# Gathers of tokens in pairs half a step apart, and one at a time for the first expert, in a fused attention and mixture-of-experts kernel

## The chip, the cores and the metric

The kernel runs on one core of one Trainium2 chip. The metric is the device time of one execution in microseconds (us), the median of three runs. A profile of one more execution gives the rows that are shown here. Engines are named as the profile names them: PE is TensorE (matmuls; PEld its weight loads), DVE is VectorE, ACT is ScalarE, POOL is GpSimd, SP is SyncE, which issues most plain DMAs.

## The reference

A banded attention (8 batches, 8 heads, 576 positions, 64 values a head; half of the heads look at 32 neighbours, half at every fourth of 128) gives 4608 tokens of 512 values. A gate picks two of eight experts for each token, and each expert is two matrix products with a ReLU between them.

```python
x = attn_out.transpose(0, 2, 1, 3).reshape(4608, 512)
noisy_logits = x @ w_gate + np.log1p(np.exp(x @ w_noise)) * noise
top2 = np.argpartition(-noisy_logits, 2, axis=1)[:, :2]
...
for e in range(8):
    for k in range(2):
        mask = top2[:, k] == e
        h = np.maximum(x[mask] @ w1[e], 0.0)       # w1[e]: 512 x 1024
        out[mask] += top2_w[mask, k, None] * (h @ w2[e])   # w2[e]: 1024 x 512
```

## The kernel before

**Stages.** The first 176 us are the attention, in half-steps ("slots"); the change leaves them alone. The attention's output `x` goes to a scratch tensor `xs` in HBM. Then come the eight experts. The first takes its tokens while the gate of the last quarter is still being worked out; the other seven are taken in the order of their load.

**One expert.** Its tokens are cut into tiles of 128, nine or ten of them, and these into three blocks of three or four tiles. For a block, `up` makes eight products (one for each 128 of the 1024 hidden values) of 12 matmuls each; ACT writes the ReLU of a product from PSUM to `hh`, DVE the remainder to `hl` (fp32 is split into two parts to be multiplied). Three PSUM buffers, named `up`, hold products that ACT and DVE have not read yet. Then `down` makes, for each tile, 24 matmuls into `dn` (two buffers), DVE scales the result to `y` (three buffers), and POOL adds `y` to the output in HBM by an indirect DMA (`scatter`). Blocks of one expert are interleaved with those of the one before.

**Tokens.** A tile's tokens are fetched by POOL with indirect DMAs (`gather`), into one of four buffers `g`. For the first expert a tile is two DMAs of 128 x 256 values; for the others four DMAs of 128 x 128, each for 32 tokens. `xsplit` turns a fetched tile round (on DVE for the seven, on PE for the first expert), ACT casts it to `x`, and DVE writes the remainder. Which tokens belong to an expert is worked out on DVE and PE by products with 0/1 matrices (`zero_one` writes `lo` and `hi`, `add_up` multiplies them into `plc`), six of them for each expert, and POOL writes the index lists `ixi`.

**Order.** The order is written out by the program. `plan(t, f)` puts a step into a heap under a due time; `tick(cols)` moves a clock by the matmul columns just issued and calls what is due, so a step lands on its engine's queue between two matmuls of the program. Every queue is in order. A position in the queue is no time yet: POOL runs ahead as far as its waits allow.

**Pacing.** `pace` puts a tiny instruction into POOL's queue: a 1x1 copy from the latest `hh` (`late["x"]`), so that POOL waits until ACT has written it, or a memset where no wait is asked for. The name of its target is `spacer`. In the kernel before, one such copy stands ahead of the four gathers of a tile, a memset ahead of every scatter, and `gpsimd.nop()` ahead of the first expert's gathers once the experts have begun. The first expert's gathers are taken by `first_blocks`, a generator that `some` advances: `new_slot(2)` allows two gathers, and `some` is planned at 34 steps of one microsecond of the program's clock. `drain` ends what is left.

Of the kernel before, what the change touches and what calls it, by code (L numbers as in the profile page):

```python
# [9 lines left out]
F32 = mybir.dt.float32  # L10
# [30 lines left out]
US_W2 = 3.0, 3.5  # L41
US_W2S = 0.5, 2.4, 8.6, 10.6
LAG = 15
US_X = (17, 46)
WIN = (0.5, 19, 23, 27, 31, 35), (0.5, 6.3, 12.1, 17.9, 23.7, 29.5)
LAGS = (6, 3.9, 3.9, 3.9, 3.9, 3.9), (5.7,) * 6

# [2 lines left out]
def attention_moe_kernel(ctx, tc, qt, kp, kd, vpl, vdl, wgn, noise, w1, w2, out, CAPS=(1184, 1216, 1216, 1184, 1184, 1152, 1152, 1152), SPLITS=(0, 384, 768)):  # L50
    nc = tc.nc
    tensor, vector, scalar, gpsimd, sync = nc.tensor, nc.vector, nc.scalar, nc.gpsimd, nc.sync
# [3 lines left out]
    TLS = [[(128 * i, min(128, cap - 128 * i)) for i in range((cap + 127) // 128)] for cap in CAPS]  # L56
# [16 lines left out]
    gp_ = ctx.enter_context(tc.tile_pool(name="gp", bufs=4))  # L73
# [239 lines left out]
    gens, early, behind = [], [True], [True]  # L313
    room, held, rate = [0], set(), [1]

    fresh, backlog, mark = [True], [], [None]

    def new_slot(scatters, speed=1):
        if scatters:
            room[0], fresh[0], mark[0] = scatters, True, late["x"]  # L320
        rate[0] = speed
        held.clear()

    def pace(yes=True, at=None):

        at = late["x"] if at is None else at
        if yes and at is not None:
            gpsimd.tensor_copy(spacer, at)  # L328
        else:
            gpsimd.memset(spacer, 0.0)  # L330

    def pool_turn():


        if experts[0]:
            gpsimd.nop()
        else:
            pace(fresh[0], mark[0])
        fresh[0] = False
        room[0] -= 1  # L340

# [5 lines left out]
    def micro(n=1):  # L347

        n = (1, n, 2 * n)[rate[0]]
        for g in list(gens):
            while n > 0 and g not in held:
                try:
                    r = next(g)
                except StopIteration:
                    gens.remove(g)
                    break
                n -= 1
                if r == 1:  # L360
                    held.add(g)
                if r == 3:
                    break
# [522 lines left out]
    GT, GOT = {}, {}  # L886

    def gather(e, t, c=None):
        r0, rn = TLS[e][t] if e != "o" else (0, 128)
        if e == 0:  # L890

            GOT[t] = c == 1
            if c == 0:
                GT[e, t] = gp_.tile([128, 4, 128], F32, name="g")
            rows = 2304 * (next((i for i in range(U - 1) if r0 + rn <= SPLITS[i]), U - 1) + 1)
            gpsimd.indirect_dma_start(
                out=GT[e, t][0:rn, 2 * c:2 * c + 2].rearrange("p c d -> p (c d)"), out_offset=None, in_=xs[0:rows],
                in_offset=bass.IndirectOffsetOnAxis(ap=IX[0][0][0:rn, t, c:c + 1], axis=0))
            return
        g = gp_.tile([128, 4, 128], F32, name="g")  # L900
        if e != "o":
            pace()
        for j in range(rn // 32):
            gpsimd.indirect_dma_start(out=g[:, j], out_offset=None, in_=xq,  # L904
                                      in_offset=bass.IndirectOffsetOnAxis(
                                          ap=IX[e][1][:, r0 // 32 + j:r0 // 32 + j + 1], axis=0))
        GT[e, t] = g
# [22 lines left out]
    def new_x(e, bi):  # L930
        pool = late["xp0" if bi == 0 else "xp"]
        t = pool.tile([128, 2, 4, NBL[bi]], F32R, name="x", tag="raw" if bi == 0 else f"x{bi}")
        X[e, bi] = (t[:, 0], t[:, 1])

    def plan_x(e, bi, t, step, lag):
        plan(t, lambda: new_x(e, bi))
        for i, ti in enumerate(range(BLS[e][bi][0], BLS[e][bi][1])):
            plan(t + step * i, lambda ti=ti: gather(e, ti))
            plan(t + step * i + lag, lambda ti=ti: xsplit(e, bi, ti), 1.2)

    HT = {}
# [116 lines left out]
    def plan(t, f, lag=None):  # L1058

        if lag is not None:  # L1060
            plan(t, lambda: plan(now[0] + lag, f()))
        else:
            heappush(due, (t, next(turn), f))
# [27 lines left out]
    experts, done = [False], [0, 0, 0]  # L1091
# [18 lines left out]
    def split_first(bi, t):  # L1110
        if GOT.get(t) and (0, t) in GT:
            xsplit(0, bi, t)()
            done[bi] += 1

    def x_block(bi):
# [4 lines left out]
        for i, t in enumerate(range(BLS[0][bi][0], BLS[0][bi][1])):  # L1120
            plan(US_X[bi - 1] + 3.0 * i, lambda t=t: split_first(bi, t))

# [44 lines left out]
    for kc in range(4):  # L1167
        a, b, c = ((-3, 2.5, 3), (-2, 4.5, 5), (2, 7.5, 8), (2, 7.5, 8))[kc]
# [61 lines left out]
        gate_turn(*f, last=2)()  # L1230
    micro(14)

    def some():
        new_slot(2)
        micro(8)

    def drain():
        while gens:
            some()


    actx.close()
# [14 lines left out]
    def dur(e, bi, dn, a=0, b=9):  # L1257
        t0, t1, s0, n = BLS[e][bi]
        st = tail(e, bi)
        if (a, b) != (0, 9):  # L1260
            n, st = 128 * (min(b, t1 - t0) - a), 0
        return (96 * n if not dn else 24 * 4 * (n - st) + 8192 * (st > 0)) / 2400.0
# [6 lines left out]
    for e in range(E):  # L1269
        first, last = e == 0, e == E - 1  # L1270
        order = [(0, 0, e), (1, 2, e - 1), (0, 1, e), (1, 0, e), (0, 2, e), (1, 1, e)]
        if first:

            order = [(0, 0, 0), (1, 0, 0), (0, 1, 0), (1, 1, 0), (0, 2, 0), (1, 2, 0)]
        elif e == 1:
            order = [(0, 0, 1), (1, 0, 1), (0, 1, 1), (0, 2, 1), (1, 1, 1)]
        t, at_ = start, {}
        for dn, bi, x, *ab in order:
            at_[dn, bi] = t
            t += dur(x, bi, dn, *ab)  # L1280
        end = t
        t = start if e < 2 else at_[0, 1]
        if not first:
            plan(t - 6, lambda e=e: (stage_w2(EID[e], 0), stage_w2(EID[e], 1)))
        turns = [US_W2[0] + US_W2[1] * c for c in range(4)] if first else US_W2S
        for c in range(4):
            plan(t + turns[c], lambda c=c: split_w2(c), 1.2)
            if c < 2 and not first:
                plan(t + turns[c] + 0.1, lambda c=c, e=e: stage_w2(EID[e], c + 2))
        if first:  # L1290
            half = late["hp"].tile([128, 8, 512], F32, name="half", tag="hh")
            for c in range(2):
                stage_w2(0, c + 2, half[:, 2 * c:2 * c + 2])
            plan(0, lambda: new_x(0, 1))

            def last_gate(before):
                while any(g in gens for g in before):
                    yield 1
                yield from gate(NT - NG, NG)
                plan(now[0] + 4, lambda: new_x(0, 2))  # L1300
                list_block(2)
                yield 0
                yield from totals()

            gens.append(last_gate([g for g in gens if g.__name__ == "turn_by_turn"]))
            for i in range(34):
                plan(start + i, some)
            plan(start + 33.5, drain)
            plan(start + 35, numbers)
            experts[0] = True  # L1310
        else:
            plan_x(e, 2, start + 2, *((7.5, 17) if e == 1 else (9, LAG)))
        if not last:
            if first:
                t = plan_places(1, start + 34.5, [3.9 * b for b in range(6)], (3.85,) * 6)
            t = max(ready.pop(0), start + 29, at_[0, 1]) if ready else t
            if e + 2 < E:
                ready.append(plan_places(e + 2, at_[1, 2] + 6 if first else at_[1, 1] + 7.5, WIN[first], LAGS[first]))
            plan_x(e + 1, 0, t, *((6, 13) if first else (9, LAG)))
            plan_x(e + 1, 1, t + (18 if first else 27), *((6, 13) if first else (9, LAG)))  # L1320
            t = at_[0, 2] + dur(e, 2, False)
            plan(t - 8, lambda e=e: (stage_w1(EID[e + 1], 0), stage_w1(EID[e + 1], 1)))
            for c in range(4):
                plan(t + 0.5 + 3 * c, lambda c=c: split_w1(c), 1.2)
                if c < 2:
                    plan(t + 0.6 + 3 * c, lambda c=c, e=e: stage_w1(EID[e + 1], c + 2))
        for dn, bi, x, *ab in order:
            if dn:
                down(x, bi, *ab)
            else:  # L1330
                while e == 0 and done[bi] < BLS[0][bi][1] - BLS[0][bi][0]:
                    some()
                    for t in range(*BLS[0][bi][0:2]):
                        split_first(bi, t)
                up((e, bi), X.pop((e, bi)), BLS[e][bi][3], tail(e, bi))
        start = end
# [7 lines left out]
    with tc.If(big > 0):  # L1344
        with tc.For_i(0, E, 1) as r:
            e = nc.values_load(ci[0:1, bass.ds(r, 1)], min_val=0, max_val=E - 1)
# [92 lines left out]
```

## Time and profile before

| | us |
|---|---|
| median of 3 runs | 1041.82 |
| lowest and highest run | 1040.22, 1042.13 |
| the profiled execution, its own time | 1046.44 |
| its span, first to last instruction | 1044.6 |
| PE busy in the span | 1007.8 |
| DVE, POOL, ACT busy | 572.1, 482.3, 319.9 |

The profiled execution took 4.62 us more than the median run, and 1.84 us of its time lie outside its span. PE is busy for 96% of the span.

### The profile page before, as it was taken

Reading aid. Unit: us, or ns where it says so; the run is one execution under the profiler, and the core shown is the slowest. Engines: PE = TensorE matmul, PEld = TensorE weight load, DVE = VectorE, ACT = ScalarE, POOL = GpSimd, SP = SyncE. Lnnn points to the kernel's source line nnn. Section 1 sums busy time; section 2 is a strip of 40 time slices with the busy share of each in tenths; the row PEclk is TensorE's granted clock in tenths of the full one; section 3 lists DMA queues with packets and bytes.
Section 4 is the critical chain, followed back from the end, with each engine's and each line's share of the span. In section 5 each row is a group of like instructions: output and inputs, shape, how many; then the busy total and the mean of one; then the engine's idle time right before and its main releaser. Section 6 shows DMA issues by size and latency. Waiting matters only on the chain.

```text
span 1044.6 us, 20009 instructions
## 1 busy us (share of the span) xinstructions
PE 1007.8 (96%) x7773; PEld 889.0 (85%) x7776; DVE 572.1 (55%) x1445; ACT 319.9 (31%) x605; POOL 482.3 (46%) x665
## 2 busy tenths in 40 slices
PE   7999999989999999999999999999999999999996
PEld 4778877888988988988988997899799988999885
DVE  6766867846486364736463557345644574444211
ACT  6765767311231231313121312232222212322010
POOL 5000020341787676565546554764376437653113
PEclk9999999999999999999999999999999999999999
DMA  7998987741364162345234433443343425344213
GB/s 307 347 346 307 313 315 259 290 99 22 74 154 94 31 142 51 86 86 112 60 74 96 94 83 54 109 93 81 50 119 80 98 47 122 82 95 90 31 18 45
DMA packets 58643, 132.03 MB, mean 126 GB/s; under 512 B 11216, under 2 KB 20944, under 8 KB 57264
## 3 DMA queue, kind: packets, MB, share of 16 engines
q1 hardware_dynamic: 38544, 92.02, 26.4%
q0 software_dynamic: 20000, 38.69, 20.9%
q8 instruction: 62, 1.02, 0.4%
q14 instruction: 37, 0.30, 0.1%
HBM read 91.93 MB, written 38.73 MB: 125 GB/s over the span
## 4 chain that ended last, share of the span: by engine, by line
PE 70%; issue 8%; DVE 7%; DMA 6%; POOL 3%; ACT 2%; another core or an unknown queue 2%; SPq 0%; POOLq 0%; DVEq 0%; ACTq 0%
PE up L985 31%; PE dn L1027 28%; DMA qt<-in_qt 2%; PE o L444 2%; PE s L397 2%; POOL g L904 2%; POOL out_rows L1004 1%; DMA out_rows<-y,ixs 1%; PE pp L426 1%; DMA xs<-x 1%; PE plc L756 1%; PE xtp L479 1%; DVE lo L745 1%; PE pp L501 1%
## 5 line engine op out<-in xcount | busy, mean ns | idle before, releaser
L985 PE MATMUL up<-x,w1h 128*128 128x384 f32 (+2 forms) x1536 | 401.2, 342 | 3.8 <-DVE hl L991 3.0
L904 POOL DMA_INDIRECT g<-xs,ixi x258 | 266.4, 1033 | 80.3 <-issue 77.2
L985 PEld LDWEIGHTS up<-x,w1h 128*128 128x128 f32 x1536 | 280.6, 189 | 8.6 <-DVE hl L991 3.3
L985 PE MATMUL up<-x,w1l 128*128 128x384 f32 (+2 forms) x768 | 262.2, 341 | 0.0
L1027 PE MATMUL dn<-w2h,hh 128*128 128x512 f32 x568 | 224.7, 396 | 0.0
L991 DVE SCALAR_TENSOR_TENSOR hl<-up,hh 128x384 fp32r<-128x384 f32 x192 | 106.7, 556 | 212.9 <-ACT hh L989 156.5
L1027 PE MATMUL dn<-w2l,hh 128*128 128x512 f32 x568 | 221.9, 391 | 0.5 <-DVE w2l L872 0.5
L1027 PE MATMUL dn<-w2h,hl 128*128 128x512 f32 x568 | 222.1, 391 | 0.0
L989 ACT ACTIVATE hh<-up 128x384 fp32r<-128x384 f32 (+2 forms) x192 | 95.2, 499 | 322.8 <-PE up L985 237.8
L1004 POOL DMA_INDIRECT out_rows<-y,ixs x66 | 105.6, 1600 | 141.2 <-DVE y L1036 103.7
L985 PEld LDWEIGHTS up<-x,w1l 128*128 128x128 f32 x768 | 145.4, 189 | 1.0
L1027 PEld LDWEIGHTS dn<-w2h,hl 128*128 128x128 f32 x568 | 107.0, 188 | 23.0
L1027 PEld LDWEIGHTS dn<-w2l,hh 128*128 128x128 f32 x568 | 107.1, 188 | 21.8 <-DVE w2l L872 0.9
L1027 PEld LDWEIGHTS dn<-w2h,hh 128*128 128x128 f32 x568 | 107.1, 189 | 20.7
L1036 DVE TENSOR_SCALAR y<-dn,ixs 128x512 f32<-128x512 f32 x62 | 46.5, 749 | 134.5 <-PE dn L1027 97.2
L926 ACT CAST x<-xr 128x512 fp32r<-128x512 f32 x67 | 40.5, 604 | 204.2 <-DVE xr L924 174.6
L763 POOL TENSOR_SCALAR ixi<-ixs 32x10 int32<-32x10 int32 (+1 forms) x112 | 35.5, 317 | 53.5 <-DVE ixs L709 43.6
L328 POOL COPY spacer<-hh 1x1 f32<-1x1 f32 x67 | 24.9, 372 | 71.9 <-ACT hh L989 71.1
L745 DVE TENSOR_TENSOR lo<-il,spob 128x384 bf16<-128x384 bf16 x84 | 46.2, 550 | 15.1 <-PE plc L756 10.8
L681 POOL TENSOR_TENSOR hi<-dat,hot 128x540 bf16<-128x540 bf16 (+1 forms) x4 | 3.5, 873 | 108.9 <-DVE dat L669 94.7
L927 DVE TENSOR_TENSOR x<-xr,x 128x512 fp32r<-128x512 f32 x67 | 44.7, 667 | 7.7 <-ACT x L926 4.9
L924 DVE STREAM_TRANSPOSE xr<-g 128x512 f32<-128x512 f32 x67 | 45.7, 682 | 1.1 <-DMA g<-xs,ixi 1.1
(239 smaller groups left out, 1053.8 us busy)
## 6 DMA issues: line engine op xcount, KB each, us to landing
ws<-in_moe_w SPq DMA_DIRECT2D x34, 512.0 KB
ws<-in_moe_w SPq DMA_DIRECT2D x112, 128.0 KB
out_rows<-zero SPq DMA_DIRECT2D x38, 256.0 KB
vd<-in_vdl SPq DMA_DIRECT2D x24, 390.0 KB
vp<-in_vpl SPq DMA_DIRECT2D x16, 585.0 KB
qt<-in_qt SPq DMA_DIRECT2D x14, 576.0 KB
xs<-x SPq DMA_DIRECT2D x24, 256.0 KB
kt<-in_kd SPq DMA_DIRECT2D x16, 320.0 KB
```

Of the source, the lines that this page charges most:

```text
L745: vector.tensor_tensor(lo[:, a:a + 3], il.unsqueeze(1).to_broadcast([128, 3, 128]), spob[:, 0, t].unsqueeze(2).to_broadcast([128, 3, 128]) ...
L763: gpsimd.tensor_scalar(xi[32 * c:32 * c + 32].rearrange("p (t g) -> p g t", g=4)[:, g, 0:n], ti[32 * g:32 * g + 32, 0:n, c // 2], 2.0, flo ...
L904: gpsimd.indirect_dma_start(out=g[:, j], out_offset=None, in_=xq, in_offset=bass.IndirectOffsetOnAxis(ap=IX[e][1][:, r0 // 32 + j:r0 // 32 ...
L924: vector.transpose(xr[:, :, 0:rn].rearrange("p c (g t) -> p g c t", t=32), g[:, 0:n].rearrange("p g (c d) -> p g c d", d=32))
L926: scalar.copy(xh[:, :, o:o + rn], xr[:, :, 0:rn])
L927: return lambda: vector.tensor_tensor(xl[:, :, o:o + rn], xr[:, :, 0:rn], xh[:, :, o:o + rn].bitcast(F32), op=OP.subtract)
L985: tensor.matmul(p[:, 0:n], lhsT=a[:, 128 * f:128 * f + 128], rhs=b[:, kc, 0:n], start=(i == 0), stop=(i == 11))
L989: scalar.activation(hh[:, f, 0:n], p[:, 0:n], AF.Relu)
L991: vector.scalar_tensor_tensor(hl[:, f, 0:m], p[:, 0:m], 0.0, hh[:, f, 0:m].bitcast(F32), op0=OP.max, op1=OP.subtract)
L1004: ins = gpsimd.indirect_dma_start(out=out, out_offset=bass.IndirectOffsetOnAxis(ap=sc[0:rn, t, 1:2], axis=0), in_=y[0:rn], in_offset=None, ...
L1027: tensor.matmul(p[0:rn], lhsT=a[:, f, o:o + rn], rhs=b[:, f % 2], start=(i == 0), stop=(i == 23))
L1036: vector.tensor_scalar(y[0:rn], p[0:rn], wsc, None, op0=OP.mult)
```

## The change

Three things change. For experts two to eight the four gathers of a tile no longer stand together: `plan_x` plans two of them at the tile's time and two half a step later, and each pair has its own `pace`. For the first expert every single gather has a `pace` ahead of it also after the attention, so that it waits for a product's `hh`. And `some` allows one gather at every second call in place of two at every call, is planned 48 times in place of 34, and `drain` no longer waits for the gathers; the times at which the first expert's second and third block are turned round (`US_X`) move by 2 and 3 us.

```diff
-US_X = (17, 46)
+US_X = (19, 49)
...
     def pool_turn():
-        if experts[0]:
-            gpsimd.nop()
-        else:
-            pace(fresh[0], mark[0])
+        pace(fresh[0], mark[0])
         fresh[0] = False
         room[0] -= 1
...
-        g = gp_.tile([128, 4, 128], F32, name="g")
+        if c:
+            g = GT[e, t]
+        else:
+            g = gp_.tile([128, 4, 128], F32, name="g")
         if e != "o":
             pace()
-        for j in range(rn // 32):
+        for j in range(rn // 32) if c is None else range(2 * c, min(2 * c + 2, rn // 32)):
...
         for i, ti in enumerate(range(BLS[e][bi][0], BLS[e][bi][1])):
-            plan(t + step * i, lambda ti=ti: gather(e, ti))
+            for c in range(2 if TLS[e][ti][1] > 64 else 1):
+                plan(t + step * (i + c / 2), lambda ti=ti, c=c: gather(e, ti, c))
             plan(t + step * i + lag, lambda ti=ti: xsplit(e, bi, ti), 1.2)
...
+    calls = count()
     def some():
-        new_slot(2)
+        new_slot(1 - next(calls) % 2)
         micro(8)
     def drain():
-        while gens:
-            some()
+        while any(g.__name__ != "first_blocks" for g in gens):
+            new_slot(0)
+            micro(8)
...
-            for i in range(34):
+            for i in range(48):
                 plan(start + i, some)
```

The first place is POOL's queue where the first expert's third block is fetched, after the second scatter of that expert. `g` are the tiles, `hh_3394` the ReLU of its first block, `hh_3824` that of its second. Before:

```order
L1004 DMA out_rows<-y_3721,ixf_1984 4864x512
L896 DMA g_3794<-xs_57,ixf_1984 128x256 x2
L896 DMA g_3811<-xs_57,ixf_1984 128x256 x2
L896 DMA g_3823<-xs_57,ixf_1984 128x256 x2
L896 DMA g_3850<-xs_57,ixf_1984 32x256 x2
L1003 MEMSET spacer_184 1x1
L1004 DMA out_rows<-y_3768,ixf_1984 4864x512
```

And of the change, from the third of the eight gathers on:

```order
L328 COPY spacer_184<-hh_3394 1x1
L893 DMA g_3840<-xs_57,ixf_1984 128x256
L328 COPY spacer_184<-hh_3824 1x1
L893 DMA g_3840<-xs_57,ixf_1984 128x256
L328 COPY spacer_184<-hh_3824 1x1
L893 DMA g_3954<-xs_57,ixf_1984 128x256
L328 COPY spacer_184<-hh_3824 1x1
L893 DMA g_3954<-xs_57,ixf_1984 128x256
L328 COPY spacer_184<-hh_3824 1x1
L893 DMA g_4001<-xs_57,ixf_1984 32x256
L328 COPY spacer_184<-hh_3824 1x1
L893 DMA g_4001<-xs_57,ixf_1984 32x256
```

Eight gathers and a scatter with nothing between them but a memset have become eight gathers with a copy ahead of each, the last five of which read the second block's `hh`, which is being written product by product; the scatter of `y_3768` follows them.

The second place is POOL's queue about the last `up` and the first `down` of the third expert (the same piece comes again for the later ones). Before:

```order
L328 COPY spacer_184<-hh_6404 1x1
L904 DMA g_6512<-xs_57,ixi_5372 128x128 x4
L1003 MEMSET spacer_184 1x1
L1004 DMA out_rows<-y_6370,ixs_4481 4864x512
L328 COPY spacer_184<-hh_6404 1x1
L904 DMA g_6595<-xs_57,ixi_5372 128x128 x4
L1003 MEMSET spacer_184 1x1
L1004 DMA out_rows<-y_6558,ixs_4481 4864x512
```

And of the change:

```order
L328 COPY spacer_184<-hh_6428 1x1
L904 DMA g_6537<-xs_57,ixi_5383 128x128 x2
L328 COPY spacer_184<-hh_6428 1x1
L904 DMA g_6537<-xs_57,ixi_5383 128x128 x2
L1004 MEMSET spacer_184 1x1
L1005 DMA out_rows<-y_6394,ixs_4484 4864x512
L328 COPY spacer_184<-hh_6428 1x1
L904 DMA g_6621<-xs_57,ixi_5383 128x128 x2
L1004 MEMSET spacer_184 1x1
L1005 DMA out_rows<-y_6584,ixs_4484 4864x512
L328 COPY spacer_184<-hh_6428 1x1
L904 DMA g_6621<-xs_57,ixi_5383 128x128 x2
```

Each four have become two and two, the second pair of the first tile has moved behind the end of `up` (its copy reads the last product's `hh`), and the second pair of the second tile stands behind the scatter of `y_6584`, which waits for the first `down` of the block.

## Rows read from the trace of the kernel before

**Rows 1.** The page: the span, and the group of the gathers of experts two to eight

```profile
span 1044.6 us, 20009 instructions
L904 POOL DMA_INDIRECT g<-xs,ixi x258 | 266.4, 1033 | 80.3 <-issue 77.2
```

**Rows 2.** PE in order of time: start, us, tile, count, idle time before and its end

```profile
226.50 0.62 PE L985 MATMUL up<-x,w1h 128*128 128x384 f32 x2 [2.97 <-DVE hl L991]
320.01 0.28 PE L756 MATMUL plc<-hi,lo 128*128 128x90 bf16 x3 [0.76 <-DVE hi L749]
361.12 0.65 PE L985 MATMUL up<-x,w1h 128*128 128x448 f32 x2 [0.81 <-issue]
406.75 0.28 PE L756 MATMUL plc<-hi,lo 128*128 128x90 bf16 x3 [0.73 <-DVE hi L749]
408.39 0.28 PE L756 MATMUL plc<-hi,lo 128*128 128x90 bf16 x3 [1.35 <-DVE hi L749]
523.25 0.28 PE L756 MATMUL plc<-hi,lo 128*128 128x90 bf16 x3 [1.27 <-DVE hi L749]
```

**Rows 3.** Who waited for whom: us in total, times, longest

```profile
DVE y L1036 <- remote: 24.2, 7, 6.9
ACT hh L989 <- remote: 20.7, 5, 7.5
...
PE plc L756 <- DVE hi L749: 7.9, 7, 1.4
```

**Rows 4.** The chain that ended last: start, us, what

```profile
215.20 2.09 PE up L985 x12
217.86 7.48 another core or an unknown queue
226.50 8.08 PE up L985 x36
...
256.83 2.27 PE up L985 x12
...
408.67 5.80 PE dn L1027 x18
414.74 4.18 PE dn L1027 x18
```

**Rows 5.** ACT and DVE in order of time, where they ran late

```profile
225.36 1.25 ACT L989 ACTIVATE hh<-up 128x384 fp32r<-128x384 f32 x3 [7.50 <-remote]
...
359.71 0.54 ACT L989 ACTIVATE hh<-up 128x448 fp32r<-128x448 f32 x1 [5.92 <-remote]
...
519.91 0.56 DVE L745 TENSOR_TENSOR lo<-il,spob 128x384 bf16<-128x384 bf16 x1 [2.18 <-PE dn L1027]
```

**Rows 6.** POOL in order of time, first and last of two strings of transfers

```profile
212.46 1.02 POOL L896 DMA_INDIRECT g<-xs,ixf  x1 [0.30 <-issue]
...
222.46 1.63 POOL L1004 DMA_INDIRECT out_rows<-y,ixf  x1 [0.22 <-issue]
...
508.37 0.97 POOL L904 DMA_INDIRECT g<-xs,ixi  x1 [0.48 <-issue]
...
519.20 0.96 POOL L904 DMA_INDIRECT g<-xs,ixi  x1 [0.30 <-issue]
```

**Rows 7.** Busy time in two stretches: PE, PEld, DVE, ACT, POOL, granted clock, DMA

```profile
227.90:231.20 3.30, 3.30 (x12) 3.30 (x11) 3.25 (x14) 0.49 (x1) 0.00 (x0) 0.50 0.18 65
408.80:412.10 3.30, 3.30 (x9) 2.61 (x8) 2.03 (x6) 0.00 (x0) 2.38 (x3) 0.50 0.14 40
```

**Rows 8.** POOL and DVE: the one tile turned round as soon as it landed

```profile
347.99 0.94 POOL L904 DMA_INDIRECT g<-xs,ixi  x1 [0.30 <-issue]
...
350.54 0.71 DVE L924 STREAM_TRANSPOSE xr<-g 128x512 f32<-128x512 f32 x1 [1.12 <-DMA g<-xs,ixi]
```

**Rows 9.** POOL, a copy between gathers that waited for nothing

```profile
444.44 0.18 POOL L328 COPY spacer<-hh 1x1 f32<-1x1 f32 x1
444.78 0.97 POOL L904 DMA_INDIRECT g<-xs,ixi  x1 [0.16 <-issue]
```

## The prediction

> **What bounds the kernel now.** I read the page first: the span is 1044.6 us [rows 1], PE is busy for 1007.8 us of it by the table above, and the chain of work that ended last runs along PE's two product lines from 176 us on. What can be gained there is PE's idle time and the time in which its clock is low. So I went through PE in order of time from 165 us to the end and kept each idle piece over half a microsecond. There are ten; the first, 0.55 us ahead of a weight remainder, has nothing to do with the gathers, the nine others are these: 2.97 us at 226.5, 0.81 at 361.1, and seven waits of `plc` for DVE's `hi` [rows 2], which the view of waits sums up as 7.9 us [rows 3]. Six of these seven are seen to belong together: 0.73 and 1.35 at 406 to 408, and one near 523, 631, 739 and 845, of which the first (1.27) is shown [rows 2].
>
> Then I asked what was late. At 215.20 PE begins the first expert's second `up`, one product every 2.09 us [rows 4], so the second product is done at 215.20 + 2 x 2.09 = 219.4. ACT reads it at 225.36, together with the next two [rows 5]: 6 us late, though ACT stood idle (7.50 us). PE, with three PSUM buffers, stops at 223.5. The view of waits calls such an end "remote", a signal whose sender it cannot tell: five times for ACT (20.7 us), seven times for DVE's `y` (24.2 us) [rows 3]. The reader is to see what POOL does meanwhile: from 212.46 to the scatter at 222.46 it issues nine indirect transfers, one every 1.25 us, with no wait between them [rows 6], and the signal comes some microseconds after that string ends. At 359.71 ACT is late in the same way [rows 5]. At 519.91 DVE's `lo` starts late on a signal of PE [rows 5], in a string that began at 508.37 and whose last gather is at 519.20 [rows 6]; `hi` follows `lo`, and PE pays 1.27 us at 523.25 [rows 2]. So PE's signals arrive late inside long strings of POOL's transfers. That is a coincidence seen many times, not a mechanism that the trace shows.
>
> **The clock.** [...] The price is in the chain: 36 `up` matmuls take 8.08 us where 12 take 2.09, so 8.08 - 6.27 = 1.81 us; 18 `dn` matmuls take 5.80 where the same take 4.18, so 1.62 us [rows 4].
>
> **The change, part by part.**
>
> *First expert.* The string of eight gathers and a scatter goes. The first three copies read an `hh` that is long written and wait for nothing; the five others wait for a product each, and products are 2.09 us apart [rows 4], so one transfer leaves per product. The last gather is issued near 229 and must be turned round and split before the third block's `up` at 256.83 [rows 4]; a gather is seen to be read 2.55 us after its issue (347.99 to 350.54) [rows 8]. More than 20 us are left, so this delay costs nothing. The scatter behind it comes some 8 us later, and its `y` buffer is asked for only in the block after. Gain if the late signal goes: 2.97 + 1.81 = 4.78 us.
>
> *Pairs.* The same 258 gathers [rows 1] leave in strings of two, and in `up` each pair waits for its own product, so POOL gets a pause between pairs: two gathers take 2.5 us, half a step is 3 to 4.5 us by the numbers with which `plan_x` is called. In `down` the copies wait for nothing, since no new `hh` is written; there the scatters, which wait for `y`, break the string. By the second place of the change the string 508.37 to 519.20 becomes a pair, a pause until the last product's `hh`, then pair, scatter, pair, a scatter that waits. Gains if the signals come in time: 0.81 us at 361.1; 0.73 + 1.35 + 1.62 = 3.70 us at 406 to 412; and the four like 523, which are 7.9 - 0.76 - 0.73 - 1.35 = 5.06 us [rows 2, 3]. The 0.76 us at 320 lie in a stretch where DVE itself is full, and I leave them.
>
> *Price on POOL.* The built program has 77 more instructions on POOL, nearly all copies. A copy that waits for nothing puts 0.34 us between two gathers (444.44 to 444.78) [rows 9] where 0.30 stand without it [rows 6]; one that waited adds 0.18 + 0.48 = 0.66 [rows 6, 9]. That is 3 to 51 us on an engine that idles 1044.6 - 482.3 = 562 us, and it holds nobody up by itself. Zero is my value; the other end comes in by the next part.
>
> *Price of later data.* The second half of a tile is planned 3 to 4.5 us later, while the turning-round keeps its place: 13 to 17 us after the first half. Ten microseconds are left in which POOL has to get to the pair, issue it (2.5 us) and land it (2.55 us). So POOL may be 5 us behind before DVE stands. It has been 4 us behind once, where DVE stood 1.12 us [rows 8] and PE lost nothing. Value: zero; the other end is below.
>
> Sum: 4.78 + 0.81 + 3.70 + 5.06 = 14.35 us. Against the profiled execution that is 1046.44 - 14.35 = 1032.1. The median of the runs is 4.62 us lower, and profiling may be part of these very stalls: then 14.35 - 4.62 = 9.73 us are left in a run, 1041.82 - 9.73 = 1032.1; if none is, 1041.82 - 14.35 = 1027.5. I take the middle: **1030 us**, own range 1026 to 1035.
>
> [...]
>
> **The rivals.**
>
> *Only the first expert is cured.* In `down` a pair's copy waits for nothing; pair, scatter, pair there are still five transfers, and it is in `down` that `plc` waits. Then 2.97 + 1.81 + 0.81 = 5.59 us are won: 1041.82 - 5.59 = 1036.2 us. For it: the late signal at 519.91 lies in such a stretch. Against: the string there was nine transfers long and had begun in `up`. Chance 0.18.
>
> *The strings are not the cause, or only under the profiler.* Signals stay late, or were never late in a run: 1041.8 us. For it: no row shows how a transfer of POOL could hold a signal of PE. Against: ACT's late hits all lie inside or right behind such strings [rows 3, 5, 6]. Chance 0.12.
>
> *Slower: the second pairs come too late.* DVE's queue is in order; when `xr` waits for a pair, the `hl` behind it waits, and ACT and PE after three products. It decides once POOL is over 5 us behind at a pair, which it can be behind a scatter that waits for a `y` from a `down` of 5.5 us, or behind the index lists. The price is that of the lateness which DVE now has near 519.91: 2.18 us of idle DVE [rows 5] made 1.27 us of PE [rows 2]. If one tile of each of three blocks of seven experts were hit so, 21 x 1.27 = 26.7 us would be lost against the 14.35 won: 1041.82 + 12.3 = 1054 us; with one tile in an expert 7 x 1.27 = 8.9 us, against only the first expert's 4.78: 1046 us, which I take. Chance 0.12.
>
> [...]
>
> **How the numbers follow.** The forecast has 0.58, the rivals 0.18, 0.12 and 0.12. The median's three runs spread by 0.18%, so 0.2% (2.1 us) is about what a measurement here can tell from no change: faster means below 1039.7. Nearly all of the first two cases is faster: 0.57 + 0.17 + 0.01 = 0.75; the same 0.13, slower 0.12. The range goes from 1026, a little under the full sum with the 0.76 us at 320 added (1026.7), up to 1041, which leaves out the slower case and half of the third: under 0.2.
>
> **What would show it.** Right: PE has no idle piece near the end of the first expert's second `up`, the granted clock stays at 1.00 after it and near 408; the five "remote" waits of ACT and the seven of `y` go from tens of microseconds to a few; `plc`'s 7.9 us for `hi` shrink to about one; POOL's busy time grows by little and its strings have two or three transfers. Second rival's sign: `plc` still waits some 1.2 us an expert. Slower: DVE's `xr` waits for `g` many times, not once. The prediction is wrong if late signals are there beside short strings, or if they go and the runs stay at 1041.

## The result, and the profile after

The change takes 1032.05 us (median of 6 runs, 1028.30 to 1034.46); the kernel before took 1041.97 us in the runs beside it (6 runs, 1040.22 to 1047.35). The ratio is 0.9888, interval 0.9859 to 0.9917. But the gain depends on the chip: on another one the same two kernels stand at 0.9993 (0.9965 to 1.0021), and the kernel before takes 1030.05 us there.

First the chip of the first traces. The page of the change, its span, its engines and the group of the gathers:

```profile
span 1032.0 us, 20122 instructions
## 1 busy us (share of the span) xinstructions
PE 1002.2 (97%) x7773; PEld 884.3 (86%) x7776; DVE 573.4 (56%) x1445; ACT 319.7 (31%) x605; POOL 499.8 (48%) x742
...
L904 POOL DMA_INDIRECT g<-xs,ixi x258 | 266.2, 1032 | 81.8 <-issue 78.4
```

A gather takes 1032 ns, where [rows 1] have 1033; POOL is busy for 17.5 us more, and the span is 12.6 us shorter.

PE of the change in order of time. After the attention these are all its idle pieces over half a microsecond (start, us, tile, count, idle time before and its end):

```profile
202.88 0.50 PE L1028 MATMUL dn<-w2l,hh 128*128 128x512 f32 x1 [0.81 <-DVE w2l L869]
317.09 0.28 PE L753 MATMUL plc<-hi,lo 128*128 128x90 bf16 x3 [0.53 <-DVE hi L746]
318.13 0.28 PE L753 MATMUL plc<-hi,lo 128*128 128x90 bf16 x3 [0.76 <-DVE hot L744]
```

Of [rows 2] only the 0.76 us near 320 is left, which the prediction left out, with 0.53 us beside it. The view of waits of the change, against [rows 3]:

```profile
DVE y L1037 <- remote: 13.7, 2, 7.1
ACT hh L990 <- remote: 5.8, 2, 3.5
...
DVE xr L924 <- DMA g<-xs,ixi: 1.3, 2, 1.1
PE plc L753 <- DVE hi L746: 1.0, 2, 0.5
```

The "remote" ends fell from 20.7 and 24.2 us to 5.8 and 13.7, `plc`'s wait from 7.9 us to 1.0, and `xr` waits for its tokens hardly more than before (1.3 us; 1.12 in [rows 8]). The 13.7 us of `y` are not the "few" that the prediction named as a sign. The two stretches of [rows 7], in the windows that answer to them (PE, PEld, DVE, ACT, POOL, granted clock, DMA):

```profile
216.00:235.00 19.00, 18.57 (x115) 18.01 (x114) 11.70 (x35) 3.92 (x8) 9.06 (x16) 1.00 0.52 116
400.00:420.00 20.00, 20.00 (x107) 15.51 (x106) 15.08 (x38) 1.24 (x2) 15.65 (x19) 1.00 0.38 66
```

PE is busy for 18.57 of 19.00 us and for all of 20.00, and its clock is 1.00 in both. To see where the time came from, read the start of the same PE instruction in several traces. Times from the first expert's first `up`:

| PE begins | before | change | before on chip 10 |
|---|---|---|---|
| first `up` (its own time) | 0 (176.33) | 0 (178.69) | 0 (177.79) |
| first expert, second `up` | 38.71 | 37.85 | 37.14 |
| first expert, second `down` | 61.36 | 55.68 | 54.97 |
| second expert, second `down` | 192.08 | 186.78 | 184.26 |
| third expert, second `up` | 250.93 | 241.61 | 239.09 |
| fourth | 359.72 | 348.98 | 346.46 |
| fifth | 467.29 | 455.17 | 452.65 |
| sixth | 574.95 | 561.36 | 558.85 |
| seventh | 677.12 | 662.18 | 659.66 |
| last `down` | 826.44 | 811.50 | 808.98 |

The gain comes in steps at the places of [rows 2]: 4.82 us at the first expert, 4.02 before the third expert's second `up`, then 1.42, 1.38, 1.47 and 1.35, and none behind the seventh expert's second `up`. The last column is the kernel before, unchanged, on another chip: it is shorter still.

The strings themselves did not all become short. Count as one string the transfers of POOL with gaps under 0.7 us between them: the kernel before has 20 strings of seven or more, with 222 of its 356 transfers, and the change has 21, with 230. The first expert's string is gone. At the place of 523 there is still one, of ten transfers, since its scatters do not wait (PE's first `down` matmul, DVE's reading of that tile, then the first gather, the first scatter and the last gather of the string):

```profile
506.17 0.39 PE L1028 MATMUL dn<-w2h,hh 128*128 128x512 f32 x1
...
512.17 0.75 DVE L1037 TENSOR_SCALAR y<-dn,ixs 128x512 f32<-128x512 f32 x1 [0.32 <-PE dn L1028]
...
507.65 1.11 POOL L904 DMA_INDIRECT g<-xs,ixi  x1 [0.48 <-issue]
...
510.68 1.61 POOL L1005 DMA_INDIRECT out_rows<-y,ixs  x1 [0.22 <-issue]
...
521.99 1.01 POOL L904 DMA_INDIRECT g<-xs,ixi  x1 [0.26 <-issue]
```

And in the kernel before:

```profile
513.13 0.39 PE L1027 MATMUL dn<-w2h,hh 128*128 128x512 f32 x1
...
521.40 0.75 DVE L1036 TENSOR_SCALAR y<-dn,ixs 128x512 f32<-128x512 f32 x1 [0.35 <-remote]
```

What changed is when the string begins: 4.76 us ahead of `down` before (508.37 in [rows 6]), 1.48 us behind its start now, because its first pair waits for the last product's `hh`. The first tile is done 5.96 us into `down`. Eight transfers of the string had been issued by then before, three are now, and DVE reads the tile 0.04 us after its end where it took 2.3 us. At the three later places like it the counts are the same, eight and three.

A reader's lateness is the time from the end of what it reads, or from the end of the reader's own work before if that is later. Of 270 reads of a product or a `down` tile, 17 are late by over 0.3 us in the kernel before (31.36 us together, 6.00 at most) and 10 in the change (14.55 us, 2.71 at most), all ten behind seven or more transfers of a string. So the change made late signals fewer, and those that are left fall where PE does not stop for them; it did not end them.

### The profile page after: what moved, and what is told of

Same layout as the page of the kernel before. It is cut to its first block, busy times and chain, and to the rows that moved or that the text cites. A ratio compares the mean times of both kernels' runs of the same rounds, so it can differ in the third digit from the quotient of the medians.

```text
span 1032.0 us, 20122 instructions
## 1 busy us (share of the span) xinstructions
PE 1002.2 (97%) x7773; PEld 884.3 (86%) x7776; DVE 573.4 (56%) x1445; ACT 319.7 (31%) x605; POOL 499.8 (48%) x742
## 4 chain that ended last, share of the span: by engine, by line
PE 78%; issue 8%; DVE 6%; POOL 3%; DMA 3%; ACT 1%; another core or an unknown queue 0%; SPq 0%; POOLq 0%; DVEq 0%; ACTq 0%
PE up L986 33%; PE dn L1028 31%; PE o L441 4%; PE s L394 3%; PE pp L423 2%; POOL out_rows L1005 1%; PE xtp L476 1%; PE pp L498 1%; PE plc L753 1%; DMA out_rows<-y,ixs 1%; POOL g L904 1%; PE dn L1022 1%; PE dn L1024 1%; PE s L383 1%; PE pp L540 1%
## 5 line engine op out<-in xcount | busy, mean ns | idle before, releaser
L904 POOL DMA_INDIRECT g<-xs,ixi x258 | 266.2, 1032 | 81.8 <-issue 78.4
L1005 POOL DMA_INDIRECT out_rows<-y,ixs x66 | 110.8, 1679 | 100.5 <-DVE y L1037 76.8
L328 POOL COPY spacer<-hh 1x1 f32<-1x1 f32 x144 | 49.6, 345 | 131.1 <-ACT hh L990 129.1
L855 DVE TENSOR_TENSOR w1l<-ws,w1h 128x1024 fp32r<-128x1024 f32 x32 | 38.8, 1222 | 16.7 <-issue 11.8
```

The source lines that it names most:

```text
L1005: ins = gpsimd.indirect_dma_start(out=out, out_offset=bass.IndirectOffsetOnAxis(ap=sc[0:rn, t, 1:2], axis=0), in_=y[0:rn], in_offset=None, ...
```

## The experiments

Results name their chip by a number; each kernel is timed beside the kernel before on the same chip. The signs to look for are the time of the kernel before, the "remote" waits, and the semaphore records that a trace holds: counted over the whole trace, 9,320 in the first trace of before and 9,931 in that of the change.

**The parts, chip 5.** `e1_first_alone` is the kernel before with the lines of the diff on the first expert:

```diff
-        if experts[0]:
-            gpsimd.nop()
-        else:
-            pace(fresh[0], mark[0])
+        pace(fresh[0], mark[0])
...
-        new_slot(2)
+        new_slot(1 - next(calls) % 2)
```

> The kernel before with the part on the first expert alone: one gather at a time, each behind a copy; experts two to eight keep their four gathers together. Theory (long strings of POOL's transfers hold back PE's signals until the string ends): PE's idle 2.97 us and the half clock behind it go, nothing else; the trace of the whole change was 4.82 us shorter than that of before over that stretch, so 1041.97 - 4.8 = 1037.2 us, ratio 0.995 to 0.996, and plc still waits for hi near 523, 631, 739 and 845. Rival (only the first expert counts, the pairs bring nothing): the whole gain, ratio 0.989.

`e2_pairs_alone` is the kernel before with the other lines:

```diff
-            plan(t + step * i, lambda ti=ti: gather(e, ti))
+            for c in range(2 if TLS[e][ti][1] > 64 else 1):
+                plan(t + step * (i + c / 2), lambda ti=ti, c=c: gather(e, ti, c))
```

> The kernel before with the pairs alone: experts two to eight as in the change, the first expert's gathers still in strings. Theory: PE keeps the idle piece of about 3 us and the half clock near 226; the stops at 406 to 412 and the four later ones go, in the traces 3.98 + 5.62 us, and some 1 us before: ratio 0.990 to 0.992. Rival (only the first expert counts): ratio 0.998 to 1.000, and plc waits as before.

`e3_pairs_together`, from the change:

```diff
-                plan(t + step * (i + c / 2), lambda ti=ti, c=c: gather(e, ti, c))
+                plan(t + step * i, lambda ti=ti, c=c: gather(e, ti, c))
```

> The whole change, but both pairs of a tile are planned at the tile's own time, each with its copy. Both copies then read the same hh, so that the second waits for nothing and the string is four transfers long again, with a copy of 0.18 us in its middle. Theory (what counts is the pause between strings): as the first-expert part alone, ratio 0.995 to 0.996, late signals back at the later experts. Rival (any instruction with a semaphore between two transfers lets the signals through): ratio as of the whole change, 0.989.

`e4_pairs_untied`, from the change:

```diff
         if e != "o":
-            pace()
+            pace(False)
```

> The whole change, but the copies ahead of the pairs of experts two to eight are memsets that wait for nothing (no tie to a product; the first expert keeps its copies). POOL then runs ahead as far as free buffers and scatters let it. Theory: strings grow to eight or more transfers without a pause, PE's signals come late more often than in the kernel before, and PE stops: ratio 0.997 to 1.005. Rival (where the pairs stand in the queue brings the gain, not their tie): ratio 0.989.

Measured: 1.0016 (0.9993 to 1.0039), 0.9988 (0.9967 to 1.0010), 0.9997 (0.9972 to 1.0021) and 1.0016 (0.9990 to 1.0042), beside a kernel before of 1028.72 us. Two of these lie in a range that was named (the second in its rival's, the fourth in its theory's), but by number only: there was nothing to win, and so the four runs do not tell the parts apart. No trace of the four has a "remote" wait of `hh` or `y`, and each holds between 14,122 and 14,165 semaphore records. The untied kernel has strings of up to 45 transfers here, and every product is read within 0.12 us. So the strings alone are not the cause.

**The change and the kernel before again, chips 0 and 10.**

> The change itself once more, timed against the kernel before, to see whether the gain belongs to the kernels or to the chip. Theory A (the strings hold PE's signals back by themselves): ratio 0.986 to 0.992 again, on any chip. Theory B (the late signals are a condition of one chip or of the recording there; the parts of the change brought nothing where no late signal was seen): ratio 0.989 only if late signals and a time near 1042 us of the kernel before are seen on this chip, and 0.998 to 1.002 if the kernel before takes some 1029 us.

0.9993 (0.9965 to 1.0021), the kernel before at 1030.05 us: theory B.

> The kernel before, unchanged, profiled once more. Theory A (its long strings hold signals back wherever it runs): PE idles 2.97 us near the first expert's second up, plc waits for hi some 7.9 us in all, ACT and DVE wait on remote, and the semaphore records in the trace are as few as before. Theory B (a condition under which the first traces were taken): with a time near 1029 us none of these is there, the strings of eight to twelve transfers are, and ACT reads every product within 0.1 us of its end.

1.0002 (0.9972 to 1.0033) on chip 10, where the kernel before takes 1028.42 us: theory B again. The trace of the kernel before there, at the place of [rows 5, 6] (ACT, then POOL, first and last of the string and the scatter):

```profile
217.26 0.49 ACT L989 ACTIVATE hh<-up 128x384 fp32r<-128x384 f32 x1 [11.36 <-PE up L985]
219.29 0.49 ACT L989 ACTIVATE hh<-up 128x384 fp32r<-128x384 f32 x1 [1.54 <-PE up L985]
221.37 0.49 ACT L989 ACTIVATE hh<-up 128x384 fp32r<-128x384 f32 x1 [1.59 <-PE up L985]
223.45 0.49 ACT L989 ACTIVATE hh<-up 128x384 fp32r<-128x384 f32 x1 [1.59 <-PE up L985]
...
212.34 1.02 POOL L896 DMA_INDIRECT g<-xs,ixf  x1 [0.30 <-issue]
...
221.15 0.87 POOL L896 DMA_INDIRECT g<-xs,ixf  x1 [0.30 <-issue]
...
222.32 1.63 POOL L1004 DMA_INDIRECT out_rows<-y,ixf  x1 [0.22 <-issue]
```

The string is the same, transfer for transfer, from 212.34 to 222.32. ACT takes a product every 2.08 us in the middle of it, where in [rows 5] it stood until 225.36. And its waits have for `plc`, in place of 7.9 us:

```profile
PE plc L756 <- DVE hi L749: 0.8, 1, 0.8
```

**More signals, chip 10.** From the kernel before:

```diff
     def tick(cols):
+        for _ in range(2):
+            j = next(probes) % 32
+            sync.dma_start(probe[0][:, j], xs[0:128, 4 * j:4 * j + 4])
         now[0] += cols / 2400.0
```

> The kernel before with two tiny loads (128 x 16 bytes of xs into a buffer nobody reads) issued by SP after every product and every quarter of a down tile, some 800 more plain transfers, each of which raises semaphores too. It leaves the string lengths as they are. Theory B1 (signals come late when strings and many other semaphore updates meet, a matter of how much there is): late reads by ACT and DVE, PE stops, time 5 to 15 us above the kernel before on the same chip. Theory B2 (a condition of the chip or of the recording that the kernel can't bring about): no late read, time within 3 us of the kernel before.

1.0063 (1.0032 to 1.0095), with no late read. PE stops once, and the trace in order of time says why (PE, then ACT):

```profile
297.50 1.01 PE L985 MATMUL up<-x,w1h 128*128 128x384 f32 x2 [3.61 <-DVE hl L991]
...
294.77 1.04 ACT L870 CAST w2h<-ws 128x1024 fp32r<-128x1024 f32 x1 [6.86 <-DMA ws<-in_moe_w]
```

The window behind it:

```profile
297.50:300.50 3.00, 3.00 (x9) 3.00 (x10) 2.96 (x6) 1.06 (x3) 2.53 (x4) 0.50 0.22 71
```

ACT waits 6.86 us for a weight, DVE's `hl` for ACT, PE for `hl`, and the clock is at half behind it. The tiny loads share SP's queue with the weights, which is the likely reason; no run tests it. The time, some 6 us up, is outside what B2 allowed and inside B1's range, but by this loss of another kind. On the question asked B2 stands: twice the semaphore updates (29,443 records) don't bring late reads about, none being over 0.12 us.

**How late may the second pair come, chip 3.** From the change, the second pair a whole step and one and a half steps behind the first:

```diff
-                plan(t + step * (i + c / 2), lambda ti=ti, c=c: gather(e, ti, c))
+                plan(t + step * (i + c), lambda ti=ti, c=c: gather(e, ti, c))
```

```diff
+                plan(t + step * (i + 1.5 * c), lambda ti=ti, c=c: gather(e, ti, c))
```

> The change with the second pair of a tile a whole step after the first (9 us by the program's clock in place of 4.5; 6 in place of 3 for the second expert), the turning-round where it was. Of the lag of 15 us some 6 are left, of which two gathers (2.5 us) and a landing (2.55 us) take 5. Theory (a price only when the pair lands after DVE comes to it, and then first out of DVE's and PE's slack): within 0.3% of the kernel before, xr waiting for g at a few tiles by a microsecond or two. Rival (each late tile costs PE at once, as the prediction's slower case has it): 7 or more tiles at 1.27 us, ratio above 1.008.

> The same with one and a half steps (13.5 us of the 15; 9 of 13 and 11.25 of 17 for the second expert), so that the pair is issued some 1.5 us before DVE's turning-round and must be late by some 3.5 us at nearly every tile of the last six experts, about 55 tiles. Theory: PE has three product buffers of 2.1 us each ahead of it, so that a DVE late by 3.5 us is mostly covered, and the first waits of PE come where two late tiles meet or where plc waits for hi: ratio 1.002 to 1.010. Rival (the prediction's price of 1.27 us of PE a late tile): 55 x 1.27 = 70 us, ratio near 1.07; and should nothing wait at all, 1.000, the issue times are not what sets the landing.

This chip is of the first kind: the kernel before takes 1042.98 us beside them, and the two traces hold 9,959 and 11,068 semaphore records. A whole step: 0.9917 (0.9887 to 0.9947), not to be told from the change's own 0.9888, which was timed at another time. The theory's 0.3% about the kernel before had left the late signals out. One and a half: 1.0485 (1.0448 to 1.0522). Of the whole step, the waits of `xr`:

```profile
DVE xr L924 <- DMA g<-xs,ixi: 22.4, 10, 3.5
```

And one idle piece of its PE, in order of time:

```profile
512.62 0.28 PE L753 MATMUL plc<-hi,lo 128*128 128x90 bf16 x3 [1.28 <-DVE hi L746]
```

Of one and a half steps, the same waits and those of `plc`:

```profile
DVE xr L924 <- DMA g<-xs,ixi: 151.3, 48, 8.2
...
PE plc L753 <- DVE hi L746: 18.1, 8, 3.4
```

And one place on its DVE:

```profile
1009.16 0.71 DVE L924 STREAM_TRANSPOSE xr<-g 128x512 f32<-128x512 f32 x1 [3.42 <-DMA g<-xs,ixi]
```

With a whole step ten tiles wait for 22.4 us, and 1.28 us of `plc`, as in [rows 2], are back once, behind a string of nine transfers. From the first `up` to the last `down` PE takes 815.47 us, 3.97 more than the change: at most 0.4 us a late tile. With one and a half steps 48 tiles wait for 151.3 us (3.15 us each), and PE takes 872.80 us, 61.3 more than the change: 1.28 us a late tile in the mean. The theory that product buffers would cover it fell. The prediction's price of 1.27 us came out as a mean, and partly by luck: it was read from one place where DVE stood 2.18 us and the clock did not fall. Here PE idles 39 us more than in the change, in some twenty places and not at 48 tiles, and its clock is at half for 34 us, which by the prediction's way of pricing is some 17 us more.

**Long strings on chip 3.** The untied kernel once more:

> The kernel with memsets in place of the waiting copies once more (its strings are up to 45 transfers long), for a chip on which the kernel before takes some 1043 us. Theory (on such a chip long strings hold PE's signals back): the first expert's gain of 4.8 us stays, as its copies stay, and the later experts lose as in the kernel before or more: ratio 0.993 to 1.010, late reads inside the long strings. Rival (on such a chip it is the place of the second pairs, not the length of strings): ratio 0.988 to 0.992, as the change. If the kernel before takes some 1029 us on this chip, the ratio is 1.00 by both, as in the earlier run.

1.0489 (1.0452 to 1.0527): 1089.18 us, where the same kernel took 1030.17 on chip 5. The kernel before is at 1035.94 us in these runs. On chip 5, ACT and a piece of POOL's string:

```profile
347.28 0.55 ACT L990 ACTIVATE hh<-up 128x448 fp32r<-128x448 f32 x1
349.62 0.55 ACT L990 ACTIVATE hh<-up 128x448 fp32r<-128x448 f32 x1 [1.79 <-PE up L986]
352.02 0.55 ACT L990 ACTIVATE hh<-up 128x448 fp32r<-128x448 f32 x1 [1.85 <-PE up L986]
...
335.44 1.03 POOL L904 DMA_INDIRECT g<-xs,ixi  x1 [0.15 <-POOL spacer L330]
...
358.90 0.95 POOL L904 DMA_INDIRECT g<-xs,ixi  x1 [0.30 <-issue]
```

The same place on chip 3: ACT, POOL and PE:

```profile
344.18 0.49 ACT L990 ACTIVATE hh<-up 128x384 fp32r<-128x384 f32 x1 [1.59 <-issue]
349.31 0.49 ACT L990 ACTIVATE hh<-up 128x384 fp32r<-128x384 f32 x1 [4.64 <-PE up L986]
...
364.12 0.54 ACT L990 ACTIVATE hh<-up 128x448 fp32r<-128x448 f32 x1 [12.40 <-remote]
...
337.95 1.03 POOL L904 DMA_INDIRECT g<-xs,ixi  x1 [0.15 <-POOL spacer L330]
...
361.26 0.95 POOL L904 DMA_INDIRECT g<-xs,ixi  x1 [0.30 <-issue]
...
365.52 1.08 PE L986 MATMUL up<-x,w1h 128*128 128x448 f32 x2 [10.92 <-ACT hh L990]
```

The window of the stop:

```profile
354.00:365.50 11.50, 0.36 (x1) 0.01 (x1) 0.81 (x3) 1.18 (x3) 6.70 (x10) 0.69 0.30 57
```

And over the whole execution, where the run on chip 5 has no such line:

```profile
ACT hh L990 <- remote: 51.7, 13, 12.4
```

One string of 19 transfers runs from 337.95 to 362.2 with no wait in it. The product that PE ended at 348.62 is read at 364.12, 1.9 us after the last gather; PE stands for 10.92 us. Sort the 270 reads of this trace by how many transfers of a string (gaps under 0.7 us) had been issued when the product or tile ended: of 184 with none to six issued no reader was late by over 0.3 us; of 86 with seven or more 31 were. On chip 5, same kernel, none at all, with 93 reads behind seven or more. The first trace of before fits less neatly: 14 late of 43 behind seven or more, but also three of 227 behind fewer, two of them by 1.31 and 2.41 us, in a string that began 0.96 us after one of eight.

**The parts once more, chip 4.**

> The part on the first expert alone once more, for a chip on which the kernel before takes 1035 us or more. Theory: the late signals of the first expert go, those of the later experts stay with plc's waits: in the traces of before and of the change this stretch was worth 4.8 us, ratio 0.994 to 0.997. Rival (only the first expert is cured and is worth the whole): ratio 0.988 to 0.991. On a chip with the kernel before near 1029 us the ratio is 1.00 by both.

> The pairs alone once more, for the same chip: the first expert's string of eight gathers and a scatter stays, with PE's idle 2.97 us and the half clock behind it; plc's four waits of 1.2 us, the stops at 406 to 412 and that at 361 go. Theory: some 10 us in the traces, ratio 0.989 to 0.994. Rival (the pairs bring nothing): 0.998 to 1.002. On a chip with the kernel before near 1029 us 1.00 by both.

The kernel before took 1029.81 us beside them, so this chip too had nothing to win: 1.0000 (0.9973 to 1.0026) and 0.9987 (0.9964 to 1.0010). Each part by itself was not run on a chip of the first kind; what each is worth there rests on the traces of before and of the change alone.

## Why the prediction was right, and where it was not

**The size.** 1030 was forecast, 1032.05 measured, inside its own range. The sum of 14.35 us was made from the trace, and the two traces differ by 14.94 us from the first `up` to the last `down`. Against it stands an attention that took 2.36 us longer in the change's trace, so that the executions differ by 1046.44 - 1033.72 = 12.72 us; the medians differ by 9.92. That profiling is part of the stalls, for which one end of the forecast takes off 4.62 us, no run shows. That there was anything to win is luck of the chip: on chip 0 the same change stands at 0.9993, and no trace from chips 4, 5 and 10 has a late read that it could cure.

**First expert.** 4.78 forecast, 4.82 found at its place, 0.29 of it given back in that `down`.

**406 to 412.** 3.70 forecast, 4.02 found, the half clock (0.50 in [rows 7]) gone with the stops. **The four like 523.** 5.06 forecast, 5.62 found, though not by the step forecast: the prediction has the string of nine become pair, pause, pair, scatter, pair and "a scatter that waits". The scatters did not wait, and ten transfers in a string came behind the pause. What the traces show in its place is the pause: it lets the string begin behind the start of `down`, so that three transfers and not eight are out when the first tile ends. That this is what brings the signal in time is argued from those two traces and not tested by a run. **361.** 0.81 forecast, 1.07 found, but the second expert before it lost 1.17 us in this trace, which no other trace of the change shows. The first `up` and `down` won 0.86 us that no step had: the trace of before has half the clock at 176.7 to 180.1, that of the change not.

**Price on POOL, price of later data.** Zero was taken. Where nothing is to win, the change stands at 0.9993 and its parts between 0.9987 and 1.0016, so both prices are within 0.4% of zero. That pairs half a step later are safe, and a whole step about the limit, is shown by two, ten and then 48 waits of `xr`; "some 5 us" of slack was the right size, and the whole step uses up 4.5 of it.

**The mechanism.** That late signals belong to long strings is shown on chip 3: without the waits between them 1089.18 - 1035.94 = 53 us are lost, and all 31 late reads lie behind seven transfers or more. But it is half of it. "Its strings have two or three transfers" did not come true either: 230 of 356 transfers still stand in strings of seven or more, and ten late reads are left in them. The step "signals arrive late inside long strings of POOL's transfers" failed as a general one: on chips 0, 4, 5 and 10 the same strings, and longer ones, hold nothing back. The prediction read a condition of one execution as a property of the kernel. Its rival that strings are not the cause, or signals never late in a run, is what four chips show, with the kernel before at 1028 to 1030 us in place of the 1041.8 that the rival had.

**Only the first expert cured.** Wrong on the first chip: two thirds of the gain lie behind it. **Second pairs too late.** It did not happen at half a step; its price held as a mean where 48 tiles were late, and was over three times too high where ten were. A gather took longer beside DVE's work: over the whole trace of before, the 86 gathers of experts two to eight with DVE at work for under a tenth of their time take 963 ns in the mean, the 77 with over seven tenths 1127. That is 0.16 us for each, little beside the 5 us of slack.

**What stays open.** What sets chip 3 apart, how a string of transfers holds a signal back there, and why only some reads behind a long string are late. The late signals go with missing semaphore records (9,320 to 11,068 where other chips' traces of these kernels hold 14,100 to 14,200); what ties the two, no run here shows. Missing records alone do not make late signals: the trace with one and a half steps lacks some 3,000 and has one read late, by 0.4 us. Every run listed here carries a recorded span, so no run tells whether an unrecorded execution on chip 3 would be slow. That the chip of the first traces was chip 3 is not known; it shows the same signs. The change itself was not timed on chip 3, and no trace of the kernel before was taken there. The kernel before took 1043.0 us there at one time and 1035.9 at another, so the condition is not a constant of that chip either.

## What to carry to other kernels

Before a stall with a "remote" sender is counted as a gain, profile the unchanged kernel on a second chip: here the same program took 1042 us on one and 1029 on others, and the gain was most of the distance between them. A wait on something the consumer makes, put between indirect transfers, is worth having all the same: it cost nothing measurable on chips 0, 4 and 5, whole or in parts, the change won 1.1% on the first, and strings without such waits cost 4.9% on chip 3. Then look in the trace for what it did: here it broke the first expert's string, and at four places only moved the start of another. And spread such transfers only as far as the reader's slack goes: 48 tiles that landed too late cost PE 1.28 us each in the mean, ten at most 0.4.

## What was not expected of the hardware

One kernel, unchanged, takes 1028.4, 1028.7, 1029.8, 1030.1, 1035.9 and 1043.0 us (medians of 11 to 35 runs) beside the experiments, each but the last two on a chip of its own, those two on chip 3. An engine can stand for 12.4 us until a signal arrives while the transfers keep their duration: a gather of experts two to eight takes 1017 ns in the mean in that trace and 1011 in the same kernel's on chip 5. And the attention alone ends anywhere from 171.9 to 178.0 us in traces taken on chip 5, while all behind it takes 852.1 to 853.5 us in those traces, though they are of four kernels: differences of a few microseconds are better read from the start of the same instruction in two traces, counted from a common one, than from the totals.
